# Attention, a squared-ReLU block and a gated convolution on one core: P of nine head pairs turned by VectorE and carried through DRAM

## The chip, the cores and the metric

The kernel runs on one core of one Trainium2 chip. The metric is the device time of one execution in microseconds (us), from runs of the whole program; a profile of one execution shows what its engines did. The engines are TensorE (PE, its weight loads PEld), VectorE (DVE), ScalarE (ACT), GpSimd (POOL) and SyncE (SP), which issues all transfers.

## What is computed

Everything is float32. B = 8 batches, H = 8 heads, S = 576 rows, head size 64.

```
scores = q k^T / 8;  keep scores >= rowmax - tau, else -1e9
attn   = softmax(scores);  x = attn v                      # x: (B, S, 512)
xk = mu_k x + (1-mu_k) x_prev;  xr = mu_r x + (1-mu_r) x_prev
y  = sigmoid(xr w_r) * (relu(xk w_k)^2 w_v)                # w_k: 512x1024, w_v: 1024x512
out = (sigmoid(conv5(y)) * (y w_val)) w_out
```

## The kernel before

The heads are taken in 32 pairs (4 per batch). A pair has nine chunks: chunk 2j + h (j = 0 to 3, h the head) is 128 query rows of one head against all 576 keys, and chunk 8 holds the last 64 rows of both heads. A chunk goes through: scores on TensorE into one of two PSUM buffers `s` (`qk`, as products of a float32r main part and a remainder), row minimum of the negated scores (`least`, VectorE), threshold (`thr`, GpSimd), exponential into `p` (`ex`, ScalarE), mask and row sum in one pass (`mask`, VectorE), then a guard and a reciprocal of the sum on VectorE and the normalisation of `p` on GpSimd (`norm`). Pairs 0 to 5 are "late": they skip the last three steps, and after the V product `x` is scaled instead (`guard_all`, `recip_all`, `widen`, `lay`, `scale`; `lay` is two or three f32 transposes on TensorE).

The V product needs P with keys on the partitions. From pair 4 on, a tile `p` (both heads of one j, 128 x 1152) is copied by a DMA into `pr` (`move`), transposed by TensorE in blocks of 128 x 128 against `ident_r` into PSUM (`tr`, `turn`), and copied by ScalarE into `pt` (`evac_main`, `evac_last`). `pt` has one buffer and holds half a pair: chunks 0 to 3, or 4 to 8. Then `av` multiplies it with v: eight products with 64 output rows (4 key blocks, 2 heads) and one wide one for the last 64 keys of both heads; `evac_x` copies the result into `x`. `p` has three buffers, `pr` two.

Beside it runs the first block (`moe1`): projections with w_k and w_v in nine slices of 512 rows, by the helper `mm3` (L751 before, L828 after), each of three float32r terms. It needs finished x, so it trails the attention, and what is left of it follows the last pair. Then `block2` does the rest.

The order of instructions is not written out. Every step is an operation of a planner (`Plan.op`) with an engine or a choice of engines, a duration, a priority key and the buffers it takes and frees; `Plan.order` plays the program through with these durations and writes each engine's stream in the order that comes out. On the chip every engine runs its stream in that order and waits on semaphores. SP's stream is one queue: a transfer that waits holds up what stands behind it.

Of the kernel before, what the change touches and what calls it, by code (L numbers as in the profile page):

```python
# [64 lines left out]
class Op:  # L65
    __slots__ = ("eng", "dur", "lat", "fn", "prio", "acq", "rel", "after", "left", "ready", "start", "idx", "got",
                 "port", "mode")


class Plan:  # L70
# [24 lines left out]
    def order(self, hop):  # L95

# [21 lines left out]
        while events:  # L118
# [11 lines left out]
            for e in ENGINES:  # L130
                while busy[e] <= now and ready[e]:
                    skipped, pick, held = [], None, None
                    while ready[e]:
# [6 lines left out]
                        if all(any(free[a] > 0 for a in t) if isinstance(t, tuple) else free[t] > 0  # L140
                               for t in x[2].acq):
# [13 lines left out]
                    if e == "pe" and mode == 1 and pick is not None and pick.mode != 1:  # L155
                        late = pick.prio + GANG
                        while ready[e]:
                            x = heapq.heappop(ready[e])
                            if x[2].mode == 1 and x[0] <= late and all(free[t] > 0 for t in x[2].acq):
# [10 lines left out]
                    for t in pick.acq:  # L170
                        if isinstance(t, tuple):
                            t = min((a for a in t if free[a] > 0), key=lambda a: since.get(a, 0.0))
                            pick.got.append(t)
# [54 lines left out]
COPY_FROM = 4  # L228
CVB = 3
GATES = {"a": 1, "b": 3}  # L230
XRS = {"a": 1, "b": 1}
MIX_EARLY, SIDE_EARLY = -36.7205, 2.0832
W_KEY, W_STEP = -0.8604, 71.1806
V_KEY, V_STEP = 38.9587, 2.2987
EXP_EARLY, MASK_EARLY, SUM_EARLY, NORM_EARLY, MOVE_EARLY, PREP_EARLY, XE_EARLY, KH_EARLY, KL_EARLY = -3.4426, 0.0367, 0.3513, 0.4532, 3.8756, 0.7807, 10.363, 1.0147, -4.2659
MORE_KEYS = ("EXP_EARLY", "MASK_EARLY", "SUM_EARLY", "NORM_EARLY", "MOVE_EARLY", "PREP_EARLY", "XE_EARLY", "KH_EARLY", "KL_EARLY")
R_AHEAD = 0
HOP, DMA_MARGIN, MARGIN = 269.8939, 482.1964, 1.011
VAL_LAG, OUT_LAG = 1.6991, 2.9796
# [12 lines left out]
ENGINES = ("dma", "pe", "dve", "act", "pool", "none")  # L252


@with_exitstack
def body(ctx, tc, qka, qkb, vp, w_k, w_v, w_r, w_val, w_out, conv_w, par, out):
# [86 lines left out]
    X_LO = {"dve": 560, "pool": 1160}  # L343
    R_LO = {"pool": 1160}
# [84 lines left out]
    v_t, v_done = {}, {}  # L429
    s_t, p_t, pr_t, pt_t, sm_t, ss_t, av_t, tps, tr_op, av_op = {}, {}, {}, {}, {}, {}, {}, {}, {}, {}  # L430
# [69 lines left out]
    def chunk(g):  # L500
# [6 lines left out]
        copied = pi >= COPY_FROM  # L507
        late = pi < LATE_PAIRS
# [28 lines left out]
        slow = 1.02  # L537
# [36 lines left out]
        def guard():  # L574
            sm = sm_t[g]
            nc.vector.tensor_scalar(out=sm[:, 3:4], in0=sm[:, 2:3], scalar1=1e-9, scalar2=1.0,
# [606 lines left out]
```

## Time and profile before

| | |
|---|---|
| median of 3 runs | 1213.65 us (1212.66 to 1215.63) |
| span of the profiled execution | 1214.2 us |
| TensorE busy | 1181.0 us, 97% |
| VectorE busy | 881.2 us, 73% |
| ScalarE busy | 859.7 us, 71% |
| GpSimd busy | 718.5 us, 59% |
| moved by DMA | 201.4 MB, engines busy 46% |

For the profiled execution itself the span from its first to its last instruction is the one time there is. Busy time is the union of an engine's instructions. Matmuls overlap in the pipeline, so the mean duration of one is more than it adds. Attention ends at about 818 us, the rest of the first block at about 922 us.

### The profile page before, as it was taken

What the parts mean: (1) busy time and instruction counts of PE and PEld (TensorE: products, weight loads), DVE (VectorE), ACT (ScalarE), POOL (GpSimd) and SP (SyncE); (2) the same over time, 40 slices, a digit from 0 to 9 for tenths busy, and PEclk for the clock granted to TensorE, in tenths of its full rate; (3) what the DMA queues carried; (4) which work ended last, traced back from release to release, by engine and by line L of the source; (5) the groups of instructions that cost most, each with busy time, mean ns of one, the idle gap of its engine ahead of it and who ended that gap; (6) DMA issues with size and microseconds to landing.
All of it is one profiled execution on the core that took longest, in us unless ns stands there. A gap on an engine that the chain in (4) does not pass through costs nothing.

```text
span 1214.2 us, 20512 instructions
## 1 busy us (share of the span) xinstructions
PE 1181.0 (97%) x6798; PEld 948.9 (78%) x6798; DVE 881.2 (73%) x1998; ACT 859.7 (71%) x1637; POOL 718.5 (59%) x960
## 2 busy tenths in 40 slices
PE   6888999999999999999999999999999999999998
PEld 4666788878888778878788778878887877888887
DVE  7999988888888788888877767732314997666650
ACT  7998977898788678778868857745536677654432
POOL 5887776688668668667765766531205755444321
PEclk9999999999999999999999999999999999999999
DMA  6445655567655675556555455325204333221111
GB/s 224 148 160 191 220 189 216 204 234 282 228 183 199 228 243 208 191 209 228 218 209 210 171 186 182 148 86 192 70 23 186 120 124 105 94 82 59 61 52 70
DMA packets 70777, 201.38 MB, mean 166 GB/s; under 512 B 8720, under 2 KB 21136, under 8 KB 68752
## 3 DMA queue, kind: packets, MB, share of 16 engines
q1 hardware_dynamic: 70672, 200.08, 45.9%
q8 instruction: 54, 0.88, 0.3%
q14 instruction: 51, 0.42, 0.1%
HBM read 91.07 MB, written 34.67 MB: 104 GB/s over the span
## 4 chain that ended last, share of the span: by engine, by line
PE 75%; DVE 7%; DMA 3%; POOL 2%; issue 2%; ACT 1%; SPq 0%; DVEq 0%; POOLq 0%; ACTq 0%
PE g L751 47%; PE s L524 11%; PE g L674 8%; PE g L608 6%; DVE g L1067 3%; PE g L677 3%; DMA pr<-p 2%; DVE y L1023 1%; DVE xf L810 1%; DMA stage<-in_w_val 1%; DVE gate L1090 1%; DMA raw<-in_qka 1%; DVE sm L549 0%; ACT p L562 0%; POOL xrl L832 0%
## 5 line engine op out<-in xcount | busy, mean ns | idle before, releaser
L549 DVE TENSOR_REDUCE sm<-s 128x1 f32<-128x576 f32 x288 | 214.3, 751 | 71.9 <-PE s L524 63.9
L571 DVE SCALAR_TENSOR_TENSOR p<-s,sm,p 128x576 f32<-128x576 f32 x288 | 231.2, 812 | 42.0 <-ACT p L562 22.0
L562 ACT ACTIVATE p<-s,sm 128x576 f32<-128x576 f32 x288 | 212.4, 749 | 43.2 <-DVE sm L549 23.5
L584 POOL TENSOR_SCALAR p<-p,sm 128x576 f32<-128x576 f32 x234 | 188.4, 809 | 81.5 <-DVE sm L581 68.6
L524 PE MATMUL s<-qkh 128*128 128x288 f32 x620 | 194.7, 330 | 5.2 <-DVE p L571 5.0
L524 PE MATMUL s<-kl,qkh 128*128 128x288 f32 x620 | 173.6, 296 | 1.2 <-DVE kl L462 1.2
L621 ACT ACTIVATE pt<-g 128x512 f32<-128x512 f32 x256 | 145.4, 603 | 33.6 <-PE g L608 31.2
L552 POOL TENSOR_SCALAR sm<-sm,gs 128x1 f32<-128x1 f32 x288 | 109.2, 381 | 87.0 <-DVE sm L549 62.9
L674 PE MATMUL g<-pt,v 128*64 128x320 f32 (+1 forms) x1024 | 138.8, 413 | 0.9 <-ACT pt L624 0.8
L524 PEld LDWEIGHTS s<-qkh 128*128 128x128 f32 x620 | 116.8, 188 | 17.2 <-DVE p L571 4.9
L608 PEld LDWEIGHTS g<-ident_r,pr 128*128 128x128 f32 (+1 forms) x1148 | 118.9, 140 | 14.5 <-ACT p L562 2.0
L608 PE MATMUL g<-ident_r,pr 128*128 128x128 f32 (+1 forms) x1148 | 123.4, 242 | 5.9 <-ACT p L562 1.4
L1067 DVE SCALAR_TENSOR_TENSOR g<-y,cw_t,g 128x128 f32<-128x128 f32 (+25 forms) x256 | 125.0, 517 | 4.2
L524 PEld LDWEIGHTS s<-kl,qkh 128*128 128x128 f32 x620 | 117.2, 189 | 8.4 <-DVE kl L462 1.4
L751 PE MATMUL g<-xkh,w_k_hi 128*128 128x512 f32 x288 | 116.4, 404 | 0.1
L751 PE MATMUL g<-kh,w_v_hi 128*128 128x512 f32 x288 | 115.5, 401 | 0.0
L751 PE MATMUL g<-xkh,w_k_lo 128*128 128x512 f32 x288 | 112.8, 392 | 0.0
L751 PE MATMUL g<-kh,w_v_lo 128*128 128x512 f32 x288 | 112.6, 391 | 0.0
L674 PEld LDWEIGHTS g<-pt,v 128*64 128x64 f32 x1024 | 68.1, 137 | 55.7 <-issue 9.3
L468 POOL TENSOR_TENSOR qkh<-raw,qkh 64x576 fp32r<-64x576 f32 x62 | 90.1, 1454 | 15.7 <-ACT qkh L458 7.0
L832 POOL TENSOR_TENSOR xrl<-xf,xrh 128x512 fp32r<-128x512 f32 x36 | 48.3, 1351 | 76.2 <-ACT xrh L829 76.0
L1032 POOL TENSOR_TENSOR yl<-y,yh 128x512 fp32r<-128x512 f32 x36 | 48.5, 1358 | 74.6 <-ACT yh L1029 74.6
(112 smaller groups left out, 2561.4 us busy)
## 6 DMA issues: line engine op xcount, KB each, us to landing
pr<-p SPq DMA_DIRECT2D x112, 576.0 KB, 3.5
raw<-in_qkb SPq DMA_DIRECT2D x31, 640.0 KB, 4.5
raw<-in_qka SPq DMA_DIRECT2D x31, 608.0 KB, 4.6
v<-in_vp SPq DMA_DIRECT2D x32, 320.0 KB, 3.3
x_d<-x SPq DMA_DIRECT2D x32, 290.0 KB, 4.1
v_d<-vo SPq DMA_DIRECT2D x36, 256.0 KB, 2.5
vt<-v_d SPq DMA_DIRECT2D x9, 1024.0 KB, 4.8
pr<-p SPq DMA_DIRECT2D x28, 288.0 KB, 2.8
```

The lines of the kernel that those rows point to most:

```text
L468: nc.gpsimd.tensor_tensor(out=t["hi"][lo_rows, qs], in0=t["raw"][lo_rows, qs], in1=t["hi"][lo_rows, qs].bitcast(F32), op=ALU.subtract)
L524: nc.tensor.matmul(s_t[g][:, hh, 0:NT], lhsT=q, rhs=k, start=(i == 0), stop=(i == len(terms) - 1))
L549: nc.vector.tensor_reduce(out=sm[:, 0:1], in_=s_t[g][:, :, 0:NT], op=ALU.min, axis=AX.XY)
L552: nc.gpsimd.tensor_scalar(out=sm_t[g][:, 1:2], in0=sm_t[g][:, 0:1], scalar1=tau_t, scalar2=1.0, op0=ALU.add, op1=ALU.mult)
L562: nc.scalar.activation(out=view(), in_=s_t[g][:, :, 0:NT], func=AF.Exp, bias=sm_t[g][:, 0:1], scale=-1.0)
L571: nc.vector.scalar_tensor_tensor(out=view(), in0=s_t[g][:, :, 0:NT], scalar=sm[:, 1:2], in1=view(), op0=ALU.is_le, op1=ALU.mult, accum_out=to)
L584: nc.gpsimd.tensor_scalar(out=view(), in0=view(), scalar1=sm_t[g][:, 3:4], scalar2=1.0, op0=ALU.mult, op1=ALU.mult)
L608: nc.tensor.transpose(o_.bitcast(F32R), in_=i_.bitcast(F32R), identity=ident_r)
L621: nc.scalar.activation(out=pt[:, head, :, q0:q0 + 128], in_=ps.rearrange("p (k q) -> p k q", k=4), func=AF.Copy)
L674: nc.tensor.matmul(acc[h * 64:h * 64 + 64, 0:n], lhsT=v[:, kc * 128 + h * 64:kc * 128 + h * 64 + 64], rhs=pt[:, h, kc, 0:n], start=(kc == ...
L751: nc.tensor.matmul(ps()[:, 0:tw], lhsT=W[w][wt][:, kc, m * 128:(m + 1) * 128].bitcast(F32R), rhs=a(at, kc), start=(i == 0 and x == 0), sto ...
L1067: nc.vector.scalar_tensor_tensor(out=f["ps"][:, x:at + w], in0=t["y"][:, c, x + k:at + w + k], scalar=cw[:, c, k:k + 1], in1=f["ps"][:, x: ...
```

## The change

Nine pairs (10, 12, 15, 17, 20, 22, 25, 27 and 30: those from 8 on with pi % 5 of 0 or 2) take another way for chunks 0 to 7. They become late pairs, so `p` is not normalised. When both heads of a j are masked, one VectorE instruction (`flip`) transposes every 32 x 32 block of `p` into `pr`. Four DMAs (`keep`), one for each group of 32 partitions, store it into a DRAM tile `u`, whose partition is the key within a block of 128. When both j of a half are stored, one DMA (`fetch`) loads 128 x 2304 into `pt`. Chunk 8 of these pairs is still moved and transposed by TensorE. In `av` their moving operand is read in pieces of 32 columns, 288 elements apart. `pt` becomes one tile of 2880 columns for all pairs.

Further: the guard may run on GpSimd or VectorE and the normalisation on GpSimd or ScalarE, as the planner finds one free; the planner's delays between engines come from a table (`HOPS`, `FREE`) in place of one number; all priority keys have new values, so the order changes throughout. (`hold` is given by no operation.)

```diff
+FLIP_NS, STORE_NS, FETCH_NS = 1380, 2250, 3100
+def turned_by_vector(pi):
+    return pi >= 8 and pi % 5 in (0, 2)
...
-HOP, DMA_MARGIN, MARGIN = 269.8939, 482.1964, 1.011
+HOP, DMA_MARGIN, MARGIN = 80.0, 1200.0, 1.011
...
+    GUARD = {"dve": 70, "pool": 240}
+    NORM = {"pool": 735, "act": 655}
...
-        copied = pi >= COPY_FROM
-        late = pi < LATE_PAIRS
+        flipped = turned_by_vector(pi)
+        copied = pi >= COPY_FROM and (not flipped or both)
+        half = c // 4 if c < 8 else 1
+        late = pi < LATE_PAIRS or flipped
...
+        def flip():
+            u = pr_t[pi, j] = pr_p.tile([128, 1152], F32, name="pr", tag="pr")
+            nc.vector.transpose(out=u.rearrange("p (b k q) -> p k b q", b=4, k=9), in_=p_t[pi, j].rearrange("p (k b q) -> p k b q", b=4, k=9))
+
+        def keep():
+            if j % 2 == 0:
+                u_d[pi, half] = dram.tile([128, 8, 288], F32, name=f"u{pi}_{half}")
+            for b in range(4):
+                nc.sync.dma_start(out=u_d[pi, half].rearrange("(k r) b n -> r k b n", k=4)[:, :, 4 * (j % 2) + b],
+                                  in_=pr_t[pi, j][32 * b:32 * b + 32, :].rearrange("r (k n) -> r k n", k=4))
+
+        def fetch():
+            t = pt_p.tile([128, 2880], F32, name="pt", tag="pt")
+            pt_t[pi, half] = t.rearrange("p (b k q) -> p b k q", k=9, q=32)
+            nc.sync.dma_start(out=t[:, 0:2304], in_=u_d[pi, half].rearrange("p b n -> p (b n)"))
...
-        if not copied:
+        if flipped and not both:
+            if head:
+                fl = chain("flip", op("dve", FLIP_NS, flip, [x for x, _ in turns] + [last.get("flip")], e - FLIP_EARLY,
+                                      acq=("pr",), rel=("p",)))
+                turns.clear()
+                kept_u.append(dma(589824, keep, (fl, last.get("keep")), e - MOVE_EARLY, rel=("pr",), more=STORE_NS - 1474))
+                chain("keep", kept_u[-1])
+            if c in (3, 7):
+                half_evs.append(chain("fetch", op("dma", FETCH_NS, fetch, kept_u + [last.get("fetch")], e - FETCH_EARLY, lat=LOAD_NS, acq=("pt",))))
+                kept_u.clear()
+        elif not copied:
             turn(*turns.pop()[1], nm, 440 * slow, "p")
...
+                if flipped:
+                    f = pt_t[pi, half][:, 0:n // 32]
+                    for kc in range(4):
+                        for h in range(2):
+                            nc.tensor.matmul(acc[h * 64:h * 64 + 64, 0:n],
+                                             lhsT=v[:, kc * 128 + h * 64:kc * 128 + h * 64 + 64],
+                                             rhs=f[:, :, 5 * h + kc, :], start=(kc == 0), stop=False)
+                    nc.tensor.matmul(acc[:, 0:n], lhsT=v[:, 512:640], rhs=f[:, :, 4, :], start=False, stop=True)
+                    return
```

Counted over the whole program, the f32r transposes go from 1120 to 796 (128 columns), the `lay` transposes from 30 to 75, VectorE's `kl` subtractions from 54 to 30 (GpSimd's from 18 to 42), SP's transfers from 411 to 537.

On TensorE, at the first half of pair 10 before: transposes (`g` from `ident_r,pr`) of its last tile, projections, scores of later chunks, then the V product from `pt` and `ptl`.

```order
L608 MATMUL g_3387<-ident_r,pr 128x128 x4
L608 MATMUL g_3393<-ident_r,pr 128x128
L751 MATMUL g_3329<-xkl,w_k_hi 128x512 x4
L524 MATMUL s<-qkh 128x288
L524 MATMUL s<-kl,qkh 128x288
L524 MATMUL s<-qkh 128x288
L524 MATMUL s<-kl,qkh 128x288
L674 MATMUL g_3414<-pt,v 64x256 x8
L677 MATMUL g_3414<-ptl,v 128x256
```

The same place now:

```order
L828 MATMUL g_3424<-xkh,w_k_hi 128x512
L828 MATMUL g_3424<-xkh,w_k_lo 128x512
L743 MATMUL g_3437<-pt,v 64x256 x8
L746 MATMUL g_3437<-pt,v 128x256
L552 MATMUL s<-qkh 128x288
L552 MATMUL s<-kl,qkh 128x288
L552 MATMUL s<-qkh 128x288
L552 MATMUL s<-kl,qkh 128x288
L796 MATMUL g_3475<-par_t,rb 128x128 x2
```

The transposes ahead of the V product are gone, and two transposes of `rb` (L796, `lay`) come behind it.

On VectorE, within pair 10 before (masks L571, guard L576, minimum L549, reciprocal L581):

```order
L581 RECIPROCAL sm<-sm 128x1
L462 SCALAR_TENSOR_TENSOR kl<-raw,gs,qkh 128x576
L571 SCALAR_TENSOR_TENSOR p,sm<-s,sm,p 128x576
L576 TENSOR_SCALAR sm<-sm 128x1
L549 TENSOR_REDUCE sm<-s 128x1
L581 RECIPROCAL sm<-sm 128x1
L549 TENSOR_REDUCE sm<-s 128x1
L810 SCALAR_TENSOR_TENSOR xf<-x,par_t,xf 128x128
L571 SCALAR_TENSOR_TENSOR p,sm<-s,sm,p 128x576
```

And now (mask L599, minimum L577, turn L683, the reciprocal of a whole half L782):

```order
L577 TENSOR_REDUCE sm<-s 128x1 x2
L599 SCALAR_TENSOR_TENSOR p,ss<-s,sm,p 128x576
L683 STREAM_TRANSPOSE pr<-p 128x9x4x32
L577 TENSOR_REDUCE sm<-s 128x1
L599 SCALAR_TENSOR_TENSOR p,ss<-s,sm,p 128x576 x2
L683 STREAM_TRANSPOSE pr<-p 128x9x4x32
L782 RECIPROCAL ss<-ss 128x4
L577 TENSOR_REDUCE sm<-s 128x1 x2
L488 SCALAR_TENSOR_TENSOR kl<-raw,gs,qkh 128x640
L599 SCALAR_TENSOR_TENSOR p,ss<-s,sm,p 128x576 x2
L683 STREAM_TRANSPOSE pr<-p 128x9x4x32
```

Behind two masks of one tile stands a turn, and the guard and reciprocal of each chunk are gone.

On SP, pair 10 before: each tile one move from `p` to `pr`, between the loads of later pairs.

```order
L638 DMA pr<-p 128x1152
L451 DMA raw<-in_qkb 128x1280
L638 DMA pr<-p 128x1152
L392 DMA stage<-in_w_r 128x512
L736 DMA x_d_67<-x 128x580
L497 DMA v<-in_vp 128x640
L638 DMA pr<-p 128x1152
L451 DMA raw<-in_qka 128x1216
L638 DMA pr<-p 128x1152
L638 DMA pr<-p 128x576
```

And now, with the stores of both tiles of the first half (`u_0`), its fetch into `pt`, and those of the second half (`u_1`):

```order
L689 DMA u_0_3166<-pr 32x4x288 x4
L427 DMA w_d_r<-stage 256x1x512
L689 DMA u_0_3166<-pr 32x4x288 x4
L477 DMA raw<-in_qka 128x1216
L417 DMA stage<-in_w_r 128x512
L689 DMA u_1_3310<-pr 32x4x288 x4
L695 DMA pt<-u_0_3166 128x2304
L813 DMA x_d_67<-x 128x580
L689 DMA u_1_3310<-pr 32x4x288 x4
L679 DMA pr<-p 128x576
L477 DMA raw<-in_qkb 128x1280
L523 DMA v<-in_vp 128x640
```

Four stores stand where one move stood, and a fetch behind them, with loads and the next half's first stores between.

## Rows read from the trace of the kernel before

**Rows 1.** Windows: us, busy time of PE, PEld, DVE, ACT, POOL, clock, DMA.

```profile
0.00:100.00 100.00, 80.56 (x526) 57.04 (x526) 89.82 (x181) 89.62 (x177) 78.10 (x123) 1.00 0.54 183
100.00:922.00 822.00, 815.24 (x5025) 658.18 (x5026) 596.78 (x1438) 608.35 (x1167) 504.78 (x727) 1.00 0.52 190
922.00:1214.20 292.20, 285.23 (x1250) 233.64 (x1248) 194.58 (x380) 161.67 (x295) 135.62 (x111) 1.00 0.27 93
```

**Rows 2.** The page's chain that ended last, by engine.

```profile
PE 75%; DVE 7%; DMA 3%; POOL 2%; issue 2%; ACT 1%; SPq 0%; DVEq 0%; POOLq 0%; ACTq 0%
```

**Rows 3.** Timeline of PE at 504 to 509 us: start, us, instruction.

```profile
504.64 0.39 PE L751 MATMUL g<-kh,w_v_hi 128*128 128x512 f32 x1
...
506.45 0.29 PE L524 MATMUL s<-qkh 128*128 128x288 f32 x1
...
507.50 0.45 PE L608 MATMUL g<-ident_r,pr 128*128 128x128 f32 x4
507.79 0.37 PE L524 MATMUL s<-qkh 128*128 128x288 f32 x1
508.00 0.29 PE L524 MATMUL s<-kl,qkh 128*128 128x288 f32 x1
...
508.39 0.55 PE L608 MATMUL g<-ident_r,pr 128*128 128x128 f32 x5
508.77 0.47 PE L751 MATMUL g<-kl,w_v_hi 128*128 128x512 f32 x1
```

**Rows 4.** Groups by shape: transposes, and those of `rb` | busy us, mean ns | idle.

```profile
L608 PE MATMUL g<-ident_r,pr 128*128 128x128 f32 x1120 | 121.5, 242 | 5.9 <-ACT p L562 1.4 <-ACT ptl L629 1.2 <-DMA pr<-p 1.2
...
L719 PE MATMUL g<-par_t,rb 128*128 128x128 f32 x30 | 5.4, 279 | 0.7 <-ACT pt L624 0.5 <-ACT pt L621 0.2
```

**Rows 5.** The page's groups: V products with 64 output rows.

```profile
L674 PE MATMUL g<-pt,v 128*64 128x320 f32 (+1 forms) x1024 | 138.8, 413 | 0.9 <-ACT pt L624 0.8
```

**Rows 6.** Timeline of PE at 151 us: `lay` of three, and what follows.

```profile
151.10 0.52 PE L719 MATMUL g<-par_t,rb 128*128 128x128 f32 x3
151.52 0.50 PE L751 MATMUL g<-xkh,w_k_hi 128*128 128x512 f32 x1
151.86 0.39 PE L751 MATMUL g<-xkh,w_k_lo 128*128 128x512 f32 x1
```

**Rows 7.** Groups by shape on VectorE, whole span.

```profile
L462 DVE SCALAR_TENSOR_TENSOR kl<-raw,gs,qkh 128x640 fp32r<-128x640 f32 x31 | 40.5, 1308 | 1.7 <-ACT qkh L454 1.5
...
L581 DVE RECIPROCAL sm<-sm 128x1 f32<-128x1 f32 x234 | 36.4, 160 | 3.6
L576 DVE TENSOR_SCALAR sm<-sm 128x1 f32<-128x1 f32 x234 | 34.0, 148 | 2.7
...
L1067 DVE SCALAR_TENSOR_TENSOR g<-y,cw_t,g 128x512 f32<-128x512 f32 x16 | 11.1, 750 | 0.0
...
L1067 DVE SCALAR_TENSOR_TENSOR g<-y,cw_t,g 128x64 f32<-128x64 f32 x16 | 4.5, 281 | 0.0
```

**Rows 8.** Groups of VectorE from 200 to 700 us.

```profile
L571 DVE SCALAR_TENSOR_TENSOR p<-s,sm,p 128x576 f32<-128x576 f32 x177 | 142.4, 813 | 29.5 <-ACT p L562 15.2 <-POOL sm L552 7.7 <-issue 2.3
...
L810 DVE SCALAR_TENSOR_TENSOR xf<-x,par_t,xf 128x192 f32<-128x192 f32 (+6 forms) x39 | 25.4, 658 | 0.7 <-POOL xf L804 0.7
L889 DVE TENSOR_TENSOR kl<-k,kh 128x512 fp32r<-128x512 f32 x27 | 22.4, 833 | 5.0 <-ACT kh L886 4.8
```

**Rows 9.** Window of 200 to 700 us, columns as in rows 1.

```profile
200.00:700.00 500.00, 497.03 (x3214) 400.14 (x3213) 411.08 (x1016) 397.55 (x772) 355.27 (x516) 1.00 0.60 216
```

**Rows 10.** DMA issues: count, KB each, median us to landing.

```profile
vt<-v_d SPq DMA_DIRECT2D x9, 1024.0 KB, 4.8
...
xt<-x_d SPq DMA_DIRECT2D x2, 1026.0 KB, 8.3
```

**Rows 11.** Tile `pr`: its DMA issue on SP (ns min/median/max), and landing.

```profile
L638 SPq DMA_DIRECT2D pr<-p x140: 464/471/746, 91.7 to 810.1; - x140
...
DMA to landing us min/median/max: 2.3/3.4/7.6
```

More of the change, by code (lines that the diff above doesn't have):

```diff
@@ L95, in order, with reach @@
     def order(self, hop):
+        def reach(e, f, hop):
+            if isinstance(f, dict):
+                return hop + max(HOPS[e][g] for g in f)
+            return SAME.get(e, 0.0) if e == f else hop + HOPS[e][f]
         free = dict(self.tokens)
@@ L131, in order @@
                 while busy[e] <= now and ready[e]:
-                    skipped, pick, held = [], None, None
+                    skipped, pick, held, kept = [], None, None, ()
                     while ready[e]:
@@ L139, in order @@
                             break
-                        if all(any(free[a] > 0 for a in t) if isinstance(t, tuple) else free[t] > 0
-                               for t in x[2].acq):
+                        if all(any(free[a] > 0 and a not in kept for a in t) if isinstance(t, tuple)
+                               else free[t] > 0 and t not in kept for t in x[2].acq):
                             if e == "dve" and x[2].port and port > now + PORT_TOL:
@@ L148, in order @@
                                 break
+                        elif x[2].hold and free["x"] > 0:
+                            kept = x[2].hold
                         skipped.append(x)
@@ L158, in order @@
                             x = heapq.heappop(ready[e])
-                            if x[2].mode == 1 and x[0] <= late and all(free[t] > 0 for t in x[2].acq):
+                            if x[2].mode == 1 and x[0] <= late and all(free[t] > 0 and t not in kept for t in x[2].acq):
                                 skipped.append((pick.prio, pick.idx, pick))
@@ L171, in order @@
                         if isinstance(t, tuple):
-                            t = min((a for a in t if free[a] > 0), key=lambda a: since.get(a, 0.0))
+                            t = min((a for a in t if free[a] > 0 and a not in kept), key=lambda a: since.get(a, 0.0))
                             pick.got.append(t)
@@ L575, in guard @@
             sm = sm_t[g]
[L576 removed]
+            by[gd.eng].tensor_scalar(out=sm[:, 3:4], in0=sm[:, 2:3], scalar1=1e-9, scalar2=1.0,
                                      op0=ALU.add, op1=ALU.mult)
@@ L583, in norm @@
         def norm():
-            nc.gpsimd.tensor_scalar(out=view(), in0=view(), scalar1=sm_t[g][:, 3:4], scalar2=1.0,
-                                    op0=ALU.mult, op1=ALU.mult)
+            if nm.eng == "act":
+                nc.scalar.activation(out=view(), in_=view(), func=AF.Copy, scale=sm_t[g][:, 3:4])
+            else:
+                nc.gpsimd.tensor_scalar(out=view(), in0=view(), scalar1=sm_t[g][:, 3:4], scalar2=1.0,
+                                        op0=ALU.mult, op1=ALU.mult)
         e = at - EARLY
@@ L629, in evac_last @@
                 nc.scalar.activation(out=pt_t[pi, c // 4][1][:, q0:q0 + 128], in_=tps[g, 1][:, 0:128], func=AF.Copy)
+            elif flipped:
+                for h in (0, 64):
+                    nc.scalar.activation(out=pt_t[pi, 1][h:h + 64, 8:10, 4, :],
+                                         in_=tps[g, 1][0:64, h:h + 64].rearrange("p (i q) -> p i q", i=2), func=AF.Copy)
             else:
@@ L659, in chunk @@
                                 acq=("pr",), rel=("p",)))
+            if flipped:
+                last["t"] = op("none", 0, lambda: None, (last.get("t"), last["fetch"]), 0)
             for _, a in turns:
@@ L685, in chunk @@
             deps = half_evs + [v_done[pi], last.get("av")]
-            o = av_op[pi, half] = op("pe", (3000 if half else 2430) * slow, av, deps, lt + AV_LATE, acq=(BANKS,),
+            o = av_op[pi, half] = op("pe", 3060 if half else 2479, av, deps, lt + AV_LATE, acq=(BANKS,),
                                      rel=("pt", "v") if half else ("pt",))
@@ L737, in chunk @@
                 x_kept[b, pp] = dma(296960, store_x, (x_done[b, pp],), at)
-    half_evs, masks, turns = [], [], []
+    half_evs, masks, turns, kept_u = [], [], [], []
     def mm3(ps, w, a, m, kcs, tw):
```

72 lines of the change are left out of this document (43 added, 29 removed).

## The prediction

> **What bounds the kernel now.** I read the stage windows first. TensorE is busy 815.2 of the 822 us between 100 and 922 us and 285.2 of 292.2 us after that; only the first 100 us leave it 19.4 us idle [rows 1]. The chain that ended last says the same: TensorE holds 75% of the span in it [rows 2]. VectorE comes next: 881 us of the three stages together [rows 1], and 82% of the steady stretch from 200 to 700 us [rows 9]. So a microsecond taken out of TensorE's stream ends the kernel about a microsecond earlier, as long as nothing else makes TensorE wait. The profiled execution's span, 1214.2 us, stands 0.55 us above the median of the runs, 1213.65, so I make the sum on the median.
>
> **TensorE: what is removed.** Each of the nine turned pairs loses the transposes of chunks 0 to 7: four groups of 4 and four groups of 5, 36 instructions (324 in all; the 5 of chunk 8 stay). The mean of 242 ns of a transpose is no price, since they overlap; starts of neighbours are. Four transposes start at 507.50 and the next score matmul at 507.79, 0.29 us; that matmul then holds the array 0.21 us, where eight undisturbed ones take 506.45 to 507.50, 0.131 us each, so the group costs another 0.08. A group of five takes 0.38 us and the same 0.08 after it [rows 3]. One pair: 4 x 0.37 + 4 x 0.46 = 3.32 us; nine: 29.9 us. Bounds: without the after-effect 4 x 0.29 + 4 x 0.38 = 2.68, nine times 24.1 us; by the union of busy time, 121.5 us for 1120 [rows 4], 324 x 0.1085 = 35.1 us.
>
> **TensorE: what is added.** The rows of a turned pair are no longer normalised before the product but after it, as pairs 0 to 5 already are: five more f32 transposes per pair, in groups of two and three. Three of them take 151.10 to 151.52, 0.42 us, and the projection matmul behind them 0.34 instead of the 0.226 us of eight undisturbed ones [rows 3, 6]; with 0.40 for two, 0.94 us a pair, 8.5 us in all. By busy time, 5.4 us for 30 [rows 4], 45 give 8.1 us. The V product keeps its matmuls; only their moving operand now lies in 32-column pieces. No matmul of the trace reads such an operand. Below, it costs nothing. Above, each piece costs what a matmul costs apart from its columns: 0.226 us for 512 columns (504.64 to 506.45 in eight) [rows 3] and 0.131 for 288 make 0.424 ns a column and leave 8.9 ns. The program's 8 small V products of a half show as 16 in the trace, 1024 for 64 halves [rows 5]; with the wide one 18 a half, and 7 or 9 extra pieces each: 288 a pair, 2592 in all, 23 us. I take nothing, because a piece changes neither the weights nor the PSUM range, and a matmul's start does both.
>
> [...]
>
> **VectorE.** Added: 36 turns of 128 x 1152. None is in the trace. By the slope of the conv tap, 750 ns at 512 and 281 at 64 columns, 1.047 ns a column, a turn takes 1.42 us; by the dearest row of one pass, 1308 ns for 640 columns, 2.35 us [rows 7]. Both read and write each element once; the second shares its time with GpSimd, which works on the same tile then, so I take 1.42. Further: 18 scalings of x with 256 columns and 18 with 64, by the same slope 0.48 and 0.28 us, and 18 short reciprocals. Removed: 81 reciprocals at 160 ns, and by the program 147 of the 234 guards at 148 ns (81 not needed, 66 now on GpSimd) and 24 of the 54 kl subtractions at 833 ns [rows 7, 8]. 51.1 + 13.7 + 2.9 - 13.0 - 21.8 - 20.0 = +12.9 us on 881: VectorE's total hardly moves. What matters is where it falls. From 200 to 700 us there are 177 masks, 19.67 pairs, so a pair takes 25.4 us and 20.9 of VectorE [rows 8, 9]. The program puts 64.4 projection matmuls into a turned pair and 38.9 into another, where 47.7 stood in each. TensorE's time of a turned pair is then 25.4 + 16.7 x 0.226 - 3.32 + 0.94 = 26.8 us, of another 23.4. VectorE's turned pair is 20.9 + 5.7 + 1.8 - 1.4 - 1.3 = 25.7, and with the L810 and L889 work that goes with 16.7 more projection matmuls, (25.4 + 22.4)/19.67/47.7 = 0.051 us each [rows 8], 26.55. It fits, by 0.25 us; the other pairs leave over 2 us. Some waits of TensorE at the score matmuls will come of this; I put 2 us for them.
>
> **ScalarE and GpSimd** cost nothing. ScalarE loses 108 copies out of PSUM and gets 70 normalisations; GpSimd loses 151 normalisations and gets 66 guards and 24 subtractions. Their cover is that both were under 80% busy in the steady stretch [rows 9], and what goes there is less than or about what goes away.
>
> **The way through DRAM** costs nothing while the V product starts late enough. A half that is ready after the mask needs a turn 1.4, four issues at about 0.47, landing 2.3 to 3.4 (the moves from `p` to `pr` with little beside them), and a fetch of 1152 KB, 4.8 to 8.3 by the loads of about that size [rows 10, 11]: 10.5 to 15 us; scores, minimum, exponential and mask stand 3.5 us ahead of it. In the program's order the V product of a turned half stands 6 to 10 score chunks behind that half's last scores, mostly 7 to 9, where 5 to 7 were usual; at 25.4/9 = 2.8 us a chunk, 8 are 22 us. That covers the 14 to 18.5 us. DMA engines: 18 fetches of 1.18 MB are 21 MB more on 201 MB, all within the stretch whose share is 0.60 [rows 9]; it rises to about 0.7. On SP's queue each fetch stands behind its stores with one to seven other issues between; only the fetch of pair 15's first half follows them directly, so what is queued behind it (a load of raw among it) waits a landing, some 3 us, and its V product is the one at 6 chunks, 17 us: there TensorE may wait a little.
>
> **Sum.** 1213.65 - 29.9 + 8.5 + 2 = 1194 us. The retuned keys change the order everywhere; TensorE's 33 us of idle time can shrink or grow by some of it, and I count them as unchanged.
>
> **Rivals.** (a) VectorE sets the pace in the turned pairs, from a turn of 1.48 us on (0.25 over four). At 2.35 a turned pair takes 30.3 us of VectorE, 3.5 over TensorE's, nine times 31 us: 1225, slower than before. For it: 82% already [rows 9]. Against: other pairs have slack, and projection work can run meanwhile. Half of it gives 1210. The Trainium skill's page "VectorE: DVE Perf Modes", section The three transpose paths, gives 311 ns for 128 x 128 on VectorE; nine times that is an estimate of 2.8 us a turn and by it 26.55 + 5.5 = 32.05 us a pair, 1241. No run here shows a turn.
> (b) Pieces cost as a start does: 1194 + 23 = 1217; from 7.6 ns a piece on the gain is gone.
> (c) The fetch comes late. Of the 18, each microsecond of lateness is 18 us: 1212. For it: the moves from p to pr, 3.4 us in the median, took up to 7.6 [rows 11], and `pt` has one buffer, so a fetch also waits for the V product of the half before. Against: the 22 us of cover.
> (d) The keys close part of the early idle time: 27 us net by busy time (35.1 - 8.1) and 6 of the 33: 1181.
>
> **How the numbers follow.** The sum holds with 0.72, in its own range from 1186 to 1203; (a) 0.12, spread from 1200 to 1225; (c) 0.08; (b) 0.04; (d) 0.04. The range 1181 to 1213 leaves out the dear ends of (a), (b) and (c). Taking 0.3%, 3.6 us, as what can be told from no change: faster 0.84, same 0.07, slower 0.09.
>
> **What would show it.** Right: 796 transposes L639 of about 0.108 us of busy time each, TensorE near 1160 us busy with about 33 us idle; turns near 1.4 us; V products of turned pairs with starts as far apart as others'. Wrong: turns above 1.5 us with TensorE waiting at score matmuls for masks; TensorE's longest waits ended by the DMA pt<-u; V products 0.1 us longer each; or more idle time in the first 100 us.

## The result, and the profile after

The changed kernel takes 1225.46 us (median of 3 runs, 1225.18 to 1225.74) against 1213.65: ratio 1.0088, 95% interval 1.0070 to 1.0106. It is slower by about 11 us; the forecast was 1194, faster.

The windows of the changed kernel, with the stages and columns of [rows 1]:

```profile
0.00:100.00 100.00, 77.66 (x485) 55.44 (x485) 88.94 (x169) 86.71 (x170) 76.92 (x115) 0.94 0.50 163
100.00:922.00 822.00, 799.78 (x4760) 637.44 (x4760) 604.71 (x1280) 612.75 (x1136) 453.74 (x724) 0.99 0.64 216
922.00:1223.70 301.70, 292.98 (x1278) 238.57 (x1277) 199.86 (x384) 160.72 (x299) 142.29 (x113) 1.00 0.28 96
sum 1223.70, PE 1170.42 PEld 931.45 DVE 893.51 ACT 860.18 POOL 672.95; mean PE 390.14 PEld 310.48 DVE 297.84 ACT 286.73 POOL 224.32
```

Two things stand here. TensorE is idle for 1223.7 - 1170.4 = 53.3 us where 33.2 were idle before, 20.1 us more, 15.4 of them in the middle stage (22.2 us, where [rows 1] give 6.8). And its busy time fell by 10.6 us only, where 21.4 were forecast. The clock column, after the busy times, tells why: 0.94, 0.99 and 1.00 instead of three times 1.00. The trace's record of the granted clock holds ten stretches at half speed (1.2 in place of 2.4 GHz), 35.3 us together; before, two with 6.6 us. If half of the 28.7 us more is lost work (an estimate), some 14 us of busy time are due to the clock, and at equal clock TensorE's busy time fell by some 25 us.

Where this is lost shows when the span is split at the first scores of pair 10, the first turned pair, and at the last scores of all. The first two parts, of the kernel before:

```profile
0.00:235.40 235.40, 213.35 (x1383) 163.10 (x1384) 206.06 (x448) 197.87 (x383) 172.64 (x260) 0.99 0.55 193
235.40:797.70 562.30, 558.15 (x3595) 451.00 (x3594) 453.26 (x1129) 443.74 (x861) 392.21 (x571) 1.00 0.57 208
```

and of the changed kernel:

```profile
0.00:236.40 236.40, 209.98 (x1350) 161.78 (x1351) 199.18 (x423) 202.14 (x391) 170.95 (x263) 0.96 0.57 194
236.40:807.50 571.10, 552.96 (x3360) 437.96 (x3359) 465.83 (x980) 441.04 (x817) 342.84 (x556) 0.99 0.72 239
```

Before a turned pair has run, TensorE is already idle 4.4 us longer (26.4 against 22.0) and at a lower clock: that is the work of the new keys, delays and choices of engine alone. From there to the last scores it is idle 18.1 us, where it was 4.2. Behind them the difference is under 2 us.

The groups by shape of the changed kernel, for what was added and removed (busy us, mean ns | idle before them):

```profile
L639 PE MATMUL g<-ident_r,pr 128*128 128x128 f32 x796 | 84.2, 245 | 4.3 <-ACT x L761 3.1 <-ACT vo L984 0.5 <-DMA pr<-p 0.4
...
L683 DVE STREAM_TRANSPOSE pr<-p 128x1152 f32<-128x1152 f32 x36 | 49.5, 1374 | 4.6 <-PE g L639 2.1 <-DMA u<-pr 1.9
...
L796 PE MATMUL g<-par_t,rb 128*128 128x128 f32 x75 | 13.7, 281 | 1.6 <-ACT pt L661 0.7 <-POOL wst L395 0.3 <-ACT pt L658 0.3
```

The 324 transposes went (1120 to 796), 45 transposes of `rb` came (30 to 75), and a turn takes 1374 ns. These terms are as forecast. What ended TensorE's waits, the longest groups first (us in total, times, longest):

```profile
PE s L552 <- DVE p L599: 11.4, 13, 2.5
PE g L641 <- ACT pt L658: 7.1, 8, 2.0
PE s L562 <- ACT qkh L505: 6.2, 1, 6.2
PE g L639 <- ACT x L761: 3.1, 2, 2.1
PE g L828 <- ACT vo L984: 2.2, 1, 2.2
PE s L552 <- DVE kl L488: 2.0, 3, 0.7
PE g L743 <- DMA u<-pr: 2.0, 1, 2.0
```

No single wait stands out. Three of the rows, 7.3 us in four waits, end at ScalarE's copies `x` and `vo` or at the fetch. (The last row names a store, but its wait ends at 588.59 us, 0.10 us after the landing of the fetch that was issued at 579.49 and took 9.0 us.) The transfers, in the view of DMA issues (count, KB each, median us to landing):

```profile
pr<-p SPq DMA_DIRECT2D x76, 576.0 KB, 3.6
u<-pr SPq DMA_DIRECT2D x144, 144.0 KB, 2.8
pt<-u SPq DMA_DIRECT2D x18, 1152.0 KB, 6.5
```

**One place, read through.** TensorE waits 2.18 us at 333.8 us. Its timeline there (start, us, instruction, count [idle before <- releaser]):

```profile
333.32 0.52 PE L639 MATMUL g<-ident_r,pr 128*128 128x128 f32 x5
336.02 0.50 PE L828 MATMUL g<-xkh,w_k_hi 128*128 128x512 f32 x1 [2.18 <-ACT vo L984]
...
338.21 0.44 PE L552 MATMUL s<-kl,qkh 128*128 128x288 f32 x1
338.45 0.44 PE L552 MATMUL s<-qkh 128*128 128x288 f32 x1
```

ScalarE's timeline just before:

```profile
331.33 0.72 ACT L590 ACTIVATE p<-s,sm 128x576 f32<-128x576 f32 x1
334.74 0.74 ACT L590 ACTIVATE p<-s,sm 128x576 f32<-128x576 f32 x1 [2.69 <-DMA pr<-p]
335.38 0.59 ACT L984 ACTIVATE vo<-g 128x512 f32<-128x512 f32 x1
```

The copy `vo`, for which TensorE waits, is queued on ScalarE behind an exponential, and this waits 2.69 us for a move `pr<-p` to land, since the tile `p` that it writes is still being read. SyncE's timeline shows what the move stood behind:

```profile
325.68 0.32 SPq L695 DMA_DIRECT2D pt<-u  x1
326.09 0.47 SPq L679 DMA_DIRECT2D pr<-p  x1
```

A fetch of 1152 KB was issued 0.41 us ahead of it. The DMA view of these two issues gives their landing, the last column:

```profile
pt<-u SPq DMA_DIRECT2D x1, 1152.0 KB, 7.6
```

```profile
pr<-p SPq DMA_DIRECT2D x1, 576.0 KB, 8.6
```

The move took 8.6 us, where the median in [rows 11] was 3.4. And from 337.1 us on TensorE runs at half speed: the score matmuls start 0.24 us apart, where [rows 3] have 0.131. The windows around that gap and two others (at 422.8 us ended by ScalarE's copy `x`, at 586.6 by the fetch), each pair the gap and what follows; the clock is the figure after POOL's busy time:

```profile
333.80:337.00 3.20, 1.02 (x5) 0.85 (x5) 1.43 (x4) 2.26 (x6) 0.46 (x1) 1.00 1.00 397
337.10:340.40 3.30, 3.30 (x15) 2.94 (x15) 1.25 (x4) 3.01 (x5) 2.75 (x4) 0.50 0.71 231
...
422.80:425.70 2.90, 0.85 (x9) 0.81 (x9) 2.30 (x5) 2.90 (x7) 0.72 (x2) 1.00 0.30 100
425.90:429.10 3.20, 3.20 (x12) 2.37 (x11) 2.21 (x6) 1.27 (x4) 1.89 (x5) 0.50 0.89 268
586.60:589.60 3.00, 1.04 (x11) 0.86 (x12) 2.67 (x7) 2.97 (x7) 2.74 (x3) 1.00 1.01 294
589.70:593.00 3.30, 3.30 (x14) 2.23 (x11) 0.77 (x1) 1.81 (x4) 0.90 (x2) 0.50 0.91 347
```

So these gaps of some 2 us are paid for twice, once as idle time and again by the 3.2 to 3.3 us at half speed behind them, in which, at half the work, some 1.6 us are lost (an estimate).

### The profile page after: what moved, and what is told of

Its sections match the earlier page's. It is cut to its first block, busy times and chain, and to the rows that moved or that the text cites. A ratio compares the mean times of both kernels' runs of the same rounds, so it can differ in the third digit from the quotient of the medians.

```text
span 1223.7 us, 19902 instructions
## 1 busy us (share of the span) xinstructions
PE 1170.4 (96%) x6519; PEld 931.4 (76%) x6519; DVE 893.5 (73%) x1833; ACT 860.2 (70%) x1604; POOL 672.9 (55%) x951
## 4 chain that ended last, share of the span: by engine, by line
PE 56%; DVE 10%; DMA 3%; ACT 3%; issue 2%; POOL 0%; ACTq 0%; DVEq 0%; SPq 0%
PE g L828 37%; PE s L552 8%; DVE g L1144 4%; PE g L751 4%; PE g L639 3%; DMA pr<-p 3%; PE g L743 2%; DVE y L1100 2%; DVE xf L887 1%; PE g L754 1%; DVE gate L1167 1%; PE g L746 1%; ACT g L876 1%; DMA u<-pr 1%; ACT p L590 1%
## 5 line engine op out<-in xcount | busy, mean ns | idle before, releaser
L599 DVE SCALAR_TENSOR_TENSOR p<-s,sm,p 128x576 f32<-128x576 f32 x288 | 229.8, 811 | 53.4 <-ACT p L590 34.1
L577 DVE TENSOR_REDUCE sm<-s 128x1 f32<-128x576 f32 x288 | 211.3, 748 | 68.5 <-PE s L552 60.9
L590 ACT ACTIVATE p<-s,sm 128x576 f32<-128x576 f32 x288 | 209.4, 744 | 72.6 <-DVE sm L577 49.6
L552 PE MATMUL s<-qkh 128*128 128x288 f32 x620 | 194.0, 330 | 11.9 <-DVE p L599 11.4
L1144 DVE SCALAR_TENSOR_TENSOR g<-y,cw_t,g 128x64 f32<-128x64 f32 (+28 forms) x256 | 124.6, 517 | 4.2
L658 ACT ACTIVATE pt<-g 128x512 f32<-128x512 f32 x184 | 101.2, 600 | 11.1 <-PE g L639 10.2
L751 PE MATMUL g<-pt,v 128*64 128x256 f32 (+1 forms) x736 | 103.1, 422 | 0.5 <-ACT pt L658 0.4
L639 PEld LDWEIGHTS g<-ident_r,pr 128*128 128x128 f32 (+1 forms) x824 | 82.2, 140 | 13.6 <-ACT x L761 3.3
L1176 POOL TENSOR_TENSOR gvl<-gate,gvh 128x512 fp32r<-128x512 f32 x36 | 45.7, 1293 | 81.3 <-ACT gvh L1173 44.5
L639 PE MATMUL g<-ident_r,pr 128*128 128x128 f32 (+1 forms) x824 | 85.9, 244 | 4.3 <-ACT x L761 3.1
L751 PEld LDWEIGHTS g<-pt,v 128*64 128x64 f32 x736 | 50.2, 140 | 42.2 <-issue 11.3
L828 PE MATMUL g<-xkl,w_k_hi 128*128 128x512 f32 x288 | 78.3, 393 | 0.0
```

Of the source, the lines that this page charges most:

```text
L552: nc.tensor.matmul(s_t[g][:, hh, 0:NT], lhsT=q, rhs=k, start=(i == 0), stop=(i == len(terms) - 1))
L577: nc.vector.tensor_reduce(out=sm[:, 0:1], in_=s_t[g][:, :, 0:NT], op=ALU.min, axis=AX.XY)
L590: nc.scalar.activation(out=view(), in_=s_t[g][:, :, 0:NT], func=AF.Exp, bias=sm_t[g][:, 0:1], scale=-1.0)
L599: nc.vector.scalar_tensor_tensor(out=view(), in0=s_t[g][:, :, 0:NT], scalar=sm[:, 1:2], in1=view(), op0=ALU.is_le, op1=ALU.mult, accum_out=to)
L639: nc.tensor.transpose(o_.bitcast(F32R), in_=i_.bitcast(F32R), identity=ident_r)
L658: nc.scalar.activation(out=pt[:, head, :, q0:q0 + 128], in_=ps.rearrange("p (k q) -> p k q", k=4), func=AF.Copy)
```

## The experiments

The theories at the outset: PLAN (the new keys and planned delays make an order that waits more), VECTOR (VectorE is full in turned pairs) and DMA (stores and fetches hold up what shares the engines). Measured times are medians, with the ratio to the kernel before on the same chip and its 95% interval. "Order unchanged" means that every instruction stands where it stands in the changed kernel.

**turn_only**: the kernel of before, with all its keys, planned delays and choices of engine, and the nine turned pairs. Two of the lines that its edit changes (the two keys of turn and fetch, which the kernel of before lacks, keep their new values):

```diff
-EARLY, QK_EARLY, T_LATE, EV_EARLY, AV_LATE = 4.4983, 3.9357, -5.068, 115.0147, 2.6669
+EARLY, QK_EARLY, T_LATE, EV_EARLY, AV_LATE = 166.8448, 0.7689, -0.6136, 186.5584, 0.3905
...
-HOP, DMA_MARGIN, MARGIN = 80.0, 1200.0, 1.011
+HOP, DMA_MARGIN, MARGIN = 269.8939, 482.1964, 1.011
```

> The kernel before with the nine turned pairs alone: its own priority keys, its single delay between engines, guard on VectorE and normalisation on GpSimd. Three theories for the lost time of the change (21 us expected off, 12 us on): PLAN, the new keys and shorter planned delays make a stream that waits in many places, turned pairs or not; VECTOR, VectorE is full in the turned pairs; DMA, the stores and fetches delay what shares the queue. PLAN: the first 112 us as before, idle time of TensorE near 25 us, time 1190 to 1203. VECTOR and DMA: the first 112 us as before, but the turned pairs lose 20 us as in the changed kernel: 1212 to 1220.

Measured: 1232.91 us, 1.0152 (1.0134 to 1.0171). Worse than the change itself: PLAN as I had put it, with the old keys as the cure, fell. With the old keys the turned pairs cost 19 us.

**keys_only**: the changed kernel without a turned pair.

```diff
-    return pi >= 8 and pi % 5 in (0, 2)
+    return False
```

> The changed kernel without turned pairs: all pairs from 4 on moved and transposed by TensorE, with the new keys, the new delays and the freer choice of engines. PLAN: the loss of the first 117 us stays and losses go on through the attention, idle time of TensorE over 40 us, time 1225 to 1245. VECTOR and DMA: only the early loss of 5 to 8 us stays, 1217 to 1222.

Measured: 1234.18 us, 1.0169 (1.0151 to 1.0187). The same matmuls as before take 20.5 us more with the new keys and delays. This order is neither that of before nor that of the changed kernel, as the planner orders anew. The first line of each page's busy times, before and then this kernel:

```profile
PE 1181.0 (97%) x6798; PEld 948.9 (78%) x6798; DVE 881.2 (73%) x1998; ACT 859.7 (71%) x1637; POOL 718.5 (59%) x960
```

```profile
PE 1190.0 (97%) x6798; PEld 954.5 (77%) x6798; DVE 869.5 (71%) x1879; ACT 913.8 (74%) x1732; POOL 693.6 (56%) x984
```

6798 matmuls both times, 9.0 us busier. Its span of 1231.9 us leaves 41.9 us idle, 8.7 more than before: the 17.7 us of span fall in about equal parts to waiting and to a slower clock (21.8 us at half speed by the record, where 6.6 stood; half of the difference, 7.6 us, is most of the 9.0).

**delays_only** and **old_delays** take the two halves of the retuning apart: the old keys with the new delays and no turned pair; the new keys with the old delays and the turned pairs.

The first has the edit of keys_only and the first of the two changes shown for turn_only (with all other keys); the second this one, and the tables HOPS and FREE at zero:

```diff
-HOP, DMA_MARGIN, MARGIN = 80.0, 1200.0, 1.011
+HOP, DMA_MARGIN, MARGIN = 269.8939, 482.1964, 1.011
```

> The kernel of before with no turned pair and its own keys, but with the new planned delays (a table by pairs of engines and a delay for buffers in place of one number) and the new choices of engine for guard and normalisation. keys_only (new keys and new delays, no turned pair) took 1234 us. If the delays cause the loss: 1226 to 1236 us here. If the keys do: 1212 to 1218 us.

> The changed kernel with its nine turned pairs and new keys, ordered by the planned delays of before. If the new delays cost the early 8 us and the clock falls: 1212 to 1218 us, with pair 5 starting near 108 us. If the keys do, and they were found for these delays: 1225 to 1240 us.

Measured: 1245.1 (1.0251, 1.0224 to 1.0277) and 1241.18 (1.0216, 1.0188 to 1.0243). Neither half by itself is the culprit; each works worse with the other half of the other kernel. All four mixtures of the two kernels' keys, delays and turned pairs came out 19 to 31 us above the kernel before. Which key costs the 20 us stays open.

**short_turn**: order unchanged, the turn replaced by a copy of the same tile on VectorE (its median is 760 ns, the turn's 1378), so that the 32 x 32 blocks stay unturned.

```diff
-nc.vector.transpose(out=u.rearrange("p (b k q) -> p k b q", b=4, k=9), in_=p_t[pi, j].rearrange("p (k b q) -> p k b q", b=4, k=9))
+nc.vector.tensor_copy(out=u, in_=p_t[pi, j])
```

> The changed kernel, every engine's order unchanged, with each of the 36 turns replaced by a plain copy of the same tile on VectorE (so the blocks are not turned), which should take about half the time. VECTOR: VectorE has over 20 us more room in the turned pairs, TensorE's waits there go, 1203 to 1212. PLAN and DMA: 1220 to 1227.

Measured: 1221.0 us, 1.0053 (1.0032 to 1.0073), 4.5 us less. The profiled executions differ by 2.5 us of span, and 1.2 of these lie between the first scores of pair 10 and of pair 31, where the turned pairs are. VECTOR is not the main cause.

**small_dma**: order unchanged, one store in place of four and an eighth of the fetch.

```diff
-            for b in range(4):
+            for b in range(1):
...
-nc.sync.dma_start(out=t[:, 0:2304], in_=u_d[pi, half].rearrange("p b n -> p (b n)"))
+nc.sync.dma_start(out=t[:, 0:288], in_=u_d[pi, half][:, 0])
...
-rhs=f[:, :, 5 * h + kc, :],
+rhs=f[:, :, 5 * h + kc, :].to_broadcast([128, n // 32, 32]),
```

> The changed kernel, every engine's order unchanged, with one store instead of four for a tile and a fetch of one eighth (288 of 2304 columns), which the V product then reads for every piece, so its result is not P times v. DMA: the traffic of the turned pairs is nearly gone and 108 issues leave SP, TensorE's waits in the turned pairs go, 1203 to 1212. PLAN and VECTOR: 1220 to 1227.

Measured: 1214.45 us, 1.0010 (0.9997 to 1.0022). 11 us come back.

**short_small**: both edits together.

> The changed kernel in its own order, with the turn replaced by a plain copy on VectorE and with the short transfers of small_dma (one store in place of four, a fetch of an eighth, the V product reading that eighth for every piece); only its time is read. If turn and transfers are links of one chain that ends at the V product, cutting both gives little more than cutting the transfers: 1211 to 1215 us. If VectorE and the transfers cost apart from one another, the gains add up: 1225.5 - 4.5 - 11.0 = 1210 us or less. If the order itself holds the rest (PLAN), then even without both the kernel does not come near 1194: over 1206 us, with 35 us of idle time of TensorE.

Measured: 1216.11 us, 1.0012 (0.9994 to 1.0031). Nothing is added: with short transfers the turn's length is worth nothing that can be seen. And even this kernel, without either cost, is 22 us above 1194.

**small_fetch**: all four stores kept, an eighth of the fetch; **half_fetch**: half of it.

The fetch of half_fetch, with the reading of one piece as in small_dma (small_fetch has 288 and 0:1):

```diff
-nc.sync.dma_start(out=t[:, 0:2304], in_=u_d[pi, half].rearrange("p b n -> p (b n)"))
+nc.sync.dma_start(out=t[:, 0:1152], in_=u_d[pi, half][:, 0:4].rearrange("p b n -> p (b n)"))
```

> The changed kernel in its own order with all four stores in full, but a fetch of an eighth of the bytes, the V product reading that eighth for every piece; only its time is read. BYTES (the fetch's 1.18 MB takes DMA time from what lands beside it): most of the 11 us that the short transfers gave is found here too, 1214 to 1218 us. QUEUE (the stores' issues and waits on SyncE delay what stands behind them, the moves from p to pr first): 1221 to 1226 us, and ScalarE's wait at the exponential for the move stays at some 17 us.

> The changed kernel in its own order with a fetch of half the bytes (four of eight pieces); as in small_fetch the V product reads one piece for all, so only the time is read. An eighth of the bytes took 1212.1 us, all of them 1225.5. BYTES (each byte of the fetch costs, by holding up what shares the DMA engines): between them by the bytes, 1212.1 + 13.4 x 3/7 = 1217.8 us. LANDING (what counts is that the fetch lands late, past some point): at one of the two ends, within 2 us.

Measured: 1212.08 us, 0.9980 (0.9965 to 0.9995), and 1214.11 us, 0.9996 (0.9982 to 1.0010). The stores cost nothing that can be seen; the fetch does, and not in proportion: the first half of it costs some 2 us, and the two intervals overlap. In small_fetch the move of the place above, issued behind the same fetch, lands after 3.9 us:

```profile
pr<-p SPq DMA_DIRECT2D x1, 576.0 KB, 3.9
pt<-u SPq DMA_DIRECT2D x1, 144.0 KB, 2.1
```

and on ScalarE's timeline the second exponential follows the first without a gap, with `vo` right behind:

```profile
329.86 1.35 ACT L590 ACTIVATE p<-s,sm 128x576 f32<-128x576 f32 x2
331.11 0.59 ACT L984 ACTIVATE vo<-g 128x512 f32<-128x512 f32 x1
```

The gaps of TensorE at 333.8, 422.8 (the one for `x`), 546.9 and 586.6 us of the changed kernel are gone in both, at the same instructions. The two stretches of small_fetch up to the last scores:

```profile
0.00:236.50 236.50, 211.27 (x1349) 162.64 (x1350) 200.72 (x423) 202.06 (x391) 170.16 (x263) 0.97 0.55 194
236.50:791.70 555.20, 544.34 (x3360) 432.96 (x3358) 466.40 (x979) 439.52 (x817) 342.57 (x556) 1.00 0.64 213
```

Before the turned pairs TensorE is idle 25.2 us, nearly as long as in the changed kernel (26.4); from there on it is 10.9 us in place of 18.1, and its clock stays at 1.00. Over the whole span 44.8 us of idle time and 16.1 at half speed remain, 11.6 and 9.4 more than before.

**one_piece**: the whole fetch and all stores, the V product reading one piece for all. It parts the two edits of the runs above.

```diff
-rhs=f[:, :, 5 * h + kc, :],
+rhs=f[:, :, 5 * h + kc, :].to_broadcast([128, n // 32, 32]),
```

> The changed kernel in its own order with every store and the whole fetch kept, but the V product reading one piece of the turned P for all pieces, as in small_fetch and half_fetch; only its time is read. It parts the two edits of those runs. If the bytes of the fetch cost the 13 us: 1223 to 1228 us here. If the product's reading of many pieces does: 1211 to 1216 us.

Measured: 1222.87 us, 1.0065 (1.0048 to 1.0083). So the bytes of the fetch are 1222.87 - 1212.08 = 10.8 us. The other 2.6 us are within the overlap of the two intervals, and the reading of pieces does not show in them: the V products take the same time in both kernels, and TensorE's idle time is the same (53.0 and 53.3 us). What differs in the two profiled executions is the time at half speed, 28.1 us here and 35.3 in the changed kernel.

**act_fetch**: the fetches on ScalarE's queue; **split_1**, **split_2**: each fetch in two halves, the second behind the next one or two transfers of SyncE.

The edit of act_fetch, then that of split_1 and split_2, which issue what is in `rest` behind the next one or two transfers of the order:

```diff
-nc.sync.dma_start(out=t[:, 0:2304], in_=u_d[pi, half].rearrange("p b n -> p (b n)"))
+nc.scalar.dma_start(out=t[:, 0:2304], in_=u_d[pi, half].rearrange("p b n -> p (b n)"))
```

```diff
-            nc.sync.dma_start(out=t[:, 0:2304], in_=u_d[pi, half].rearrange("p b n -> p (b n)"))
+            def piece(b):
+                nc.sync.dma_start(out=t[:, 288 * b:288 * b + 1152],
+                                  in_=u_d[pi, half][:, b:b + 4].rearrange("p b n -> p (b n)"))
+            piece(0)
+            rest.append(lambda: piece(4))
```

> The changed kernel with the 18 fetches issued by ScalarE in place of SyncE, at the same place of the program's order, all bytes kept. QUEUE (on SyncE's queue the moves from p to pr and the loads wait behind the 1.18 MB of a fetch): the exponential's waits for these moves shrink from 17 to below 10 us and the time falls to 1213 to 1219 us. BYTES (the sixteen engines carry the same bytes whichever queue they stand in): 1223 to 1229 us, or more, as ScalarE then waits for the stores to land (some 17 us of such waits stand on SyncE now).

> The changed kernel, all work and bytes kept, with each fetch in two halves of 0.59 MB: the second is issued behind the next transfer of SyncE's order instead of with the first. half_fetch lost 2 us to small_fetch and the whole fetch 13.4. LANDING (a transfer is hurt only when it comes in the middle of a long fetch): 1214 to 1220 us. BYTES: 1223 to 1228 us.

> As split_1, with the second half of the fetch two transfers behind the first. LANDING: as split_1 or up to 2 us less, 1213 to 1219 us. BYTES: 1223 to 1228 us. If the second half comes too late for the V product, TensorE waits there for the fetch and the time is over 1228 us.

Measured: 1225.92 us, 1.0098 (1.0069 to 1.0127); 1223.45, 1.0075 (1.0060 to 1.0090); 1255.61, 1.0341 (1.0315 to 1.0366). Another queue changes nothing, and the exponential's waits for moves, 17.3 us in the changed kernel, stay at 15.6. At the place above the fetch now stands on ScalarE's queue (at 327.45 us) and the move on SyncE's, 0.10 us later, and the move lands as late as it did behind the fetch:

```profile
pt<-u ACTq DMA_DIRECT2D x1, 1152.0 KB, 8.6
pr<-p SPq DMA_DIRECT2D x1, 576.0 KB, 8.7
```

So it is not the place in SyncE's queue. That it is the time of the DMA engines is what is left, and their share, 0.91 from 322 to 334.8 us of the changed kernel, fits it. The Trainium skill, "DMA: Bandwidth & Descriptors", section Queues, rings and completion order, has each DMA engine take turns between the queues that have work for it. These rows show only that neither queue waited for the other to end (the landings are 0.2 us apart); they do not show the turns, and leave open why the move, with half the bytes, lands no earlier. Splitting trades one lateness for another: in split_1 the V product waits for the second half, 7.2 us in three waits, which the changed kernel has not; in split_2 it is 15.3 us in six.

**old_small_fetch**: turn_only with an eighth of the fetch, as in small_fetch.

> The kernel of before with its own keys and delays and the nine turned pairs (turn_only, 1232.9 us), with a fetch of an eighth and the V product reading that eighth for every piece; only its time is read. If the fetch costs on this order what it costs on the new one, 13.4 us: 1219.5 us, and the rest of the distance to 1194 is the order that the old keys make once turned pairs are in it. If the fetch was the whole trouble there: 1194 to 1200 us.

Measured: 1224.53 us, 1.0077 (1.0062 to 1.0092). There too the fetch costs, 8.4 us. It stays some 10 us above the kernel before, where TensorE's sum would take 21 off. That the order holds this is the theory that is left; it is not shown.

**five_pairs**: pairs 10, 15, 20, 25 and 30 turned.

```diff
-    return pi >= 8 and pi % 5 in (0, 2)
+    return pi >= 8 and pi % 5 == 0
```

> The changed kernel with five turned pairs (10, 15, 20, 25, 30) in place of nine, ordered anew with the same keys and delays. No turned pair took 1234.2 us, nine took 1225.5. If each turned pair brings its 2.4 us of TensorE's stream less its 1.5 us of fetch whatever stands around it: 1229.4 us, within 3. If the order that the planner makes anew decides more than the pairs do: off by more than 5 us to either side.

Measured: 1234.02 us, 1.0159 (1.0142 to 1.0176), 4.6 us above the even share: between the two answers. Five turned pairs take as long as none (1234.18), and the other four bring 8.6 us: a sum by pairs is off by about 5 us once the planner orders anew.

No run of the whole computation beat the kernel before; small_fetch, which leaves seven eighths of the fetch out, is 0.2% under it.

## Why the prediction was wrong

Two steps failed. (1) "The retuned keys change the order everywhere ... I count them as unchanged": without a turned pair the new keys and delays cost 20.5 us (keys_only). In the order of the changed kernel itself a loss of that kind stands too: 4.4 us more idle time and a lower clock before the first turned pair, and in small_fetch 11.6 us more idle time and, as half of the 9.4 us more at half speed, some 4.7 of slower clock (an estimate), 16.3 us in all. What stands before the first turned pair is shown to be the order's; that the rest is, keys_only makes likely. (2) "The way through DRAM costs nothing": the fetch's bytes cost 10.8 us (one_piece against small_fetch).

With the TensorE sum as forecast, 1213.65 + 20.5 - 21.4 + 10.8 = 1223.6, where 1225.46 was measured. This comes out nearly by construction, as each kernel is measured against the one before it; the one thing tested is the -21.4. Nor are these parts the only ones: with the old keys the turned pairs cost 19 us, 8.4 of them for the fetch.

In the terms of the sum, the "2 us for TensorE's waits" were 20.1 us of idle time and some 14.3 of slower clock, against 24.9 out of the work at equal clock: 20.1 + 14.3 - 24.9 = 9.5, the difference of the two spans. One sign of being wrong came true as well: the first 100 us are idle for 22.3 us, where [rows 1] give 19.4.

**TensorE's sum held.** -29.9 + 8.5 = -21.4 was forecast. small_fetch against keys_only, the same keys and delays with and without turned pairs, differs by 1212.08 - 1234.18 = -22.1, with an eighth of the fetch still in it. These are two orders, so that the close agreement is in part luck; by busy time at equal clock the changed kernel is 24.9 us lower, between the forecast's sum and its figure by busy time, 27 (both estimates). The transposes are 0.106 us of busy time each (84.2 for 796), as put.

**The V product in pieces.** 0 was taken, 23 us the bound. At full clock 16 products of 256 columns take as long as before. First the kernel before, then a turned half:

```profile
561.51 1.95 PE L674 MATMUL g<-pt,v 128*64 128x256 f32 x16
```

```profile
267.87 1.95 PE L743 MATMUL g<-pt,v 128*64 128x256 f32 x16
```

Those of 320 columns take 2.37 us in both. Rival (b) is out: pieces of 32 f32 cost nothing here.

**VectorE.** 1.42 us for a turn, 1.374 measured; total 893.9 us forecast (881 + 12.9), 893.5 measured. By the estimate from "VectorE: DVE Perf Modes", The three transpose paths, of the Trainium skill it would have been 2.8 us; the trace is half of that. The page's 311 ns is for bf16, and the turn is f32; the measurement decides. Rival (a) did not come true: cutting the turn to 0.76 us saves 1.2 us in the turned stretch and nothing that can be seen once the fetch is short.

**The DRAM chain.** Its links landed as put: stores 2.8 us, the fetch 6.5 in the median (4.8 to 8.3 was taken), and the share of the DMA engines from 200 to 700 us rose to 0.73 ("about 0.7"). The V product waited once for the fetch itself, 2.0 us: rival (c) was nearly nothing too. What I missed is who else is late. I costed a transfer by whether its own user waits. Its 1.18 MB instead held up the moves, a move holds its `p`, the exponential that wants `p` stands ahead of `vo`, `x` and `pt` on ScalarE, and TensorE waits for those. That chain is shown in rows at one place; over the runs the exponential's waits for moves go along with it (17.3 us in the changed kernel, 20.0 in one_piece, 9.5 in small_fetch, 11.4 in half_fetch). A run that breaks this chain alone, with a further buffer of `p`, was not made.

**The clock** was in no term. TensorE was granted half speed for 6.6 us before, 21.8 in keys_only and 35.3 after. In the changed kernel each of the four single waits of 1.96 to 2.55 us between 100 and 600 us was followed by such a stretch. It is no rule: in short_turn the clock stayed at 1.00 behind waits of 2.67 us (to 547.4 us) and 1.95 (to 587.6). **ScalarE and GpSimd** are no busier, as put (860.2 and 673.0 us, before 859.7 and 718.5). But ScalarE, whose waits the forecast left out, is the link through which late moves reach TensorE.

**Left open:** which keys cost the 20 us; why the old keys with turned pairs are no better (old_small_fetch 1224.5); why half a fetch costs some 2 us and the other half 9.

## What to carry to other kernels

When a change comes with a new order, cost the order as a term of its own with a range taken from the kernel's slack, since here it weighed as much as the whole edit. Ask of an added transfer not only whether its own reader waits, but which transfers that share the engines land later, which buffers they hold, and what is queued in order behind the first instruction that wants such a buffer. In a stream that is 97% busy, allow for nearly twice the length of a new wait of TensorE of about 2 us: behind four of them here a stretch at half speed followed, though not behind every such wait.

## What was unexpected of the hardware

The same gaps do not always bring the same fall. The changed kernel and small_fetch both wait 0.75, 0.46, 1.08 and 1.67 us at four score matmuls between 273 and 282 us. The windows of 272 to 282.4 and 282.5 to 285.8 us, first of the changed kernel:

```profile
272.00:282.40 10.40, 6.45 (x39) 4.90 (x38) 8.76 (x22) 9.12 (x18) 9.28 (x15) 1.00 0.94 315
282.50:285.80 3.30, 3.30 (x14) 1.54 (x16) 3.13 (x8) 2.94 (x5) 2.18 (x4) 0.50 0.07 27
```

and of small_fetch:

```profile
272.00:282.40 10.40, 6.45 (x39) 5.01 (x37) 8.94 (x22) 8.94 (x18) 9.21 (x15) 1.00 0.66 231
282.50:285.80 3.30, 3.30 (x23) 1.84 (x22) 3.08 (x8) 2.94 (x5) 2.27 (x4) 1.00 0.03 6
```

6.45 us busy of 10.40 in both, then 0.50 in one and 1.00 in the other. The 16 V products that follow, one row in each timeline, show the price, 4.06 against 2.38 us:

```profile
282.39 4.06 PE L743 MATMUL g<-pt,v 128*64 128x320 f32 x16
```

```profile
282.56 2.38 PE L743 MATMUL g<-pt,v 128*64 128x320 f32 x16
```

So whether a gap is paid for twice is not fixed by its length alone.
